# Folding 64-bit weights with ScalarE's low bits written as 32-bit integers, sines and arctangents as separate operations, and a new recorded order, in an attention and rational-activation kernel on one core

## The chip, the core and the metric

The kernel runs on one core of a Trainium2 chip. The core has a matrix engine (TensorE, PE in the profile; PEld is its weight load), a vector engine (VectorE, DVE), a scalar engine (ScalarE, ACT), a general engine (GpSimd, POOL), and a queue that issues most transfers (SyncE, SP). Each takes its instructions in order and waits on semaphores for the others. The metric is device time of one execution in microseconds (us); lower is better.

## What is computed

A gated linear attention over 768 positions (4 batches, 8 heads, 48 channels), with a complex decay per position and channel, feeds a feed-forward layer whose activation is a ratio of two polynomials. Cut to what matters:

```
mag = sqrt(a_re^2 + a_im^2); scale = min(mag, 0.999) / (mag + 1e-6)
for t in range(768):                       # per batch and head
    S = a[t] * scale[t] * S + k[t] v[t]^T  # complex decay, 48 x 48 state
    y[t] = q[t] . real(S)
h = x @ w_in                               # x = y as 3072 x 384; w_in 384 x 2048
P = a0 + a1 h + a2 h^2 + a3 h^3
Q = 1 + |b0| |h| + |b1| h^2
out = (P / (Q + 1e-6)) @ w_out             # w_out 2048 x 384
```

The kernel gets `w_in` and `w_out` as 64-bit floats and takes each to 32 bits itself.

## The kernel before

The sequence is cut into 6 chunks of 128 positions; a chunk of one batch is a unit, 24 in all, taken in 12 pairs. For a pair, `norm` (L444), `angle` (L474) and `trig` (L496) turn the decays into running magnitudes and angles: roots, scans, an arctangent, sums of angles, sines and cosines. `outer` (L512) multiplies q and k with them, and sends the products `Q` through twelve transfers a pair into the tile `HQ`, which has channels on partitions. `attn` (L542) transposes (L555), computes scores (L566), values (L582) and states (L597) on PE; the result `xT` goes to `ffn` (L614), eight groups a pair: PE makes `ph` (L627), ACT and DVE evaluate the activation through tiles A1, A2, A3 and z into `g`, and PE sums `po` (L645). The activation's quotient uses a reciprocal square root (`ROOT`) on ACT, whose table is another than the one with sine and arctangent, so an `ACT_TABLE_LOAD` stands between them.

Ahead of this, `weights` (L405) takes 28 blocks of 64-bit weights to 32 bits with `fold` (L390): 12 of `w_in`, 512 wide, and 16 of `w_out`, 384 wide. A block arrives in a buffer `raw` (ring `g` with 4 buffers, or `wh0` to `wh2`) as pairs of 32-bit words, low and high. Before, a fold is four instructions: ACT's `Abs` of the high word into the weight tile (L398, shown as L343); the sign alone left in the high word, on DVE or POOL (L399, shown as L331); the top three bits of the low word written beside it as a 16-bit number, on ACT (L401) or DVE (L402); and one DVE operation that shifts the tile left by 3 and ors in the high word (L403, shown as L331). In each, the source or the target has one element per 8 bytes. The first `ffn` block needs the first blocks of `w_in`, and all folds have to be done in its course.

`rouse` (L603) puts matmuls without use between those of the first pairs (L609), so that PE has work there. The first two pairs (`WHOLE`) multiply in 32 bits; after `split` (L416) the weights stand as a high and a low part.

Instructions are registered in a `Plan` (L82) with engines that may run them (`ways`), and a table `ORDER` (L223) fixes in one sequence which comes when and on which engine. `list_schedule` (L131), the planner with costs, is not run while the table fits. Every `vec` instruction has line L331, every `scal` one L343, every scaled copy of `evac` or `line` on ACT L337; so the tiles tell them apart. At the end `values_ok` (L867) and `count` (L890) check what the fast path relied on; the result `bad` is loaded by all engines (L907), which then go to the slow path or to the end.

## Time and profile before

| | |
|---|---|
| three runs | 645.45, 649.0, 650.76 us; median 649.0 |
| the profiled execution | 647.0 us, of which its span 645.3 us |
| PE busy | 574.8 us (89%) |
| DVE busy | 573.4 us (89%) |
| ACT busy | 539.5 us (84%) |
| POOL busy | 220.2 us (34%) |
| mean granted TensorE clock | 0.988 |

The page takes one execution. Busy shares are means over stages with different limits, so stretches of the span are read apart: the stage ahead of the first `ffn` block (to 76.4 us), the two pairs in 32 bits (to 190 us), the steady pairs after them, and the end. The idle time before an instruction is put down to what came last. Matmuls are pipelined and their ends modelled.

### The profile page before, as it was taken

What the parts mean: (1) busy time and instruction counts of PE and PEld (TensorE: products, weight loads), DVE (VectorE), ACT (ScalarE), POOL (GpSimd) and SP (SyncE); (2) the same over time, 40 slices, a digit from 0 to 9 for tenths busy, and PEclk for the clock granted to TensorE, in tenths of its full rate; (3) what the DMA queues carried; (4) which work ended last, traced back from release to release, by engine and by line L of the source; (5) the groups of instructions that cost most, each with busy time, mean ns of one, the idle gap of its engine ahead of it and who ended that gap; (6) DMA issues with size and microseconds to landing.
All of it is one profiled execution on the core that took longest, in us unless ns stands there. A gap on an engine that the chain in (4) does not pass through costs nothing.

```text
span 645.3 us, 13131 instructions
## 1 busy us (share of the span) xinstructions
PE 574.8 (89%) x5028; PEld 531.9 (82%) x5028; DVE 573.4 (89%) x996; ACT 539.5 (84%) x902; POOL 220.2 (34%) x202
## 2 busy tenths in 40 slices
PE   0037899998999999999999899999999999999994
PEld 0026776776779999999999899989999999999993
DVE  8787899899999999989999999988999978887683
ACT  7997999898888888989989788878788797667781
POOL 1001142326448555353541442644323443010200
PEclk9997999998999999999999999999999999999998
DMA  8677514744063253561441723600440534400001
GB/s 301 236 213 185 169 46 106 158 92 100 25 136 107 74 107 74 91 140 56 82 104 58 148 90 66 131 34 27 123 107 19 132 58 103 78 2 27 0 25 30
DMA packets 39094, 62.27 MB, mean 96 GB/s; under 512 B 4464, under 2 KB 26224, under 8 KB 39024
## 3 DMA queue, kind: packets, MB, share of 16 engines
q1 hardware_dynamic: 39024, 61.36, 39.0%
q8 instruction: 41, 0.67, 0.4%
q14 instruction: 29, 0.24, 0.1%
HBM read 37.75 MB, written 4.72 MB: 66 GB/s over the span
## 4 chain that ended last, share of the span: by engine, by line
DVE 26%; PE 21%; ACT 14%; issue 5%; DMA 2%; POOL 1%; SPq 0%; ACTq 0%; DVEq 0%; POOLq 0%
DVE A L331 11%; PE po L645 8%; PE ph L627 8%; ACT z L343 5%; ACT A L343 4%; DVE z L331 4%; PE at L566 2%; PE at L582 2%; DVE g L331 2%; DVE MM L331 1%; PE at L597 1%; DVE ST L331 1%; DVE T L331 1%; DVE RU L331 1%; ACT L343 1%
## 5 line engine op out<-in xcount | busy, mean ns | idle before, releaser
L645 PE MATMUL po<-wh,g 128*128 128x384 f32 x640 | 179.9, 340 | 0.4 <-DVE g L331 0.4
L627 PE MATMUL ph<-xT,wiH 128*128 128x256 f32 x960 | 162.2, 287 | 0.9 <-DVE A L331 0.8
L331 DVE SCALAR_TENSOR_TENSOR A<-A,co,z 128x512 f32<-128x512 f32 x176 | 130.9, 743 | 27.4 <-ACT z L343 24.7
L645 PE MATMUL po<-wo,g 128*128 128x384 f32 x428 | 146.5, 385 | 3.5 <-DVE g L331 3.5
L627 PEld LDWEIGHTS ph<-xT,wiH 128*128 128x128 f32 x960 | 135.7, 190 | 3.7 <-DVE A L331 2.3
L627 PE MATMUL ph<-xT,wi 128*128 128x256 f32 x632 | 122.7, 312 | 0.6 <-ACT A L343 0.5
L645 PEld LDWEIGHTS po<-wh,g 128*128 128x128 f32 x640 | 117.0, 188 | 3.1 <-issue 1.8
L331 POOL TENSOR_TENSOR g<-A,g 128x512 fp32r<-128x512 f32 x47 | 63.8, 1359 | 140.4 <-ACT g L692 77.3
L343 ACT ACTIVATE z<-A,co 128x512 f32<-128x512 f32 x96 | 66.3, 690 | 48.5 <-DVE A L331 44.3
L627 PEld LDWEIGHTS ph<-xT,wi 128*128 128x128 f32 x632 | 99.6, 190 | 7.0 <-ACT A L343 0.9
L645 PEld LDWEIGHTS po<-wo,g 128*128 128x128 f32 x428 | 80.1, 189 | 17.6 <-DVE g L331 4.6
L331 DVE SCALAR_TENSOR_TENSOR A<-A,co,ph 128x512 f32<-128x512 f32 x96 | 70.8, 740 | 2.6 <-ACT A L343 2.3
L343 ACT ACTIVATE A<-A,co 128x512 f32<-128x512 f32 x96 | 69.3, 722 | 2.2
L331 DVE SCALAR_TENSOR_TENSOR z<-A,z 128x512 f32<-128x512 f32 x96 | 66.7, 694 | 2.6
L343 ACT ACTIVATE A<-ph,co 128x512 f32<-128x512 f32 x96 | 64.7, 681 | 4.8 <-DVE A L331 3.8
L343 ACT ACTIVATE A<-ph 128x512 f32<-128x512 f32 x96 | 56.9, 592 | 4.6 <-PE ph L627 2.3
L566 PE MATMUL at<-HQ 96*128 96x128 f32 x384 | 51.9, 283 | 6.6 <-ACT kT L337 6.0
L343 ACT ACTIVATE z<-z 128x512 f32<-128x512 f32 x96 | 56.1, 584 | 1.8
L566 PEld LDWEIGHTS at<-HQ 96*128 96x128 f32 x384 | 48.8, 197 | 9.0 <-ACT kT L337 7.4
L609 PE MATMUL po<-Q,cmask 128*128 128x256 f32 x28 | 9.7, 489 | 42.2 <-DVE Q L331 42.2
L331 POOL TENSOR_TENSOR RU<-MM,RU 128x384 f32<-128x384 f32 x13 | 13.7, 1051 | 88.3 <-DVE RU L331 88.3
L609 PEld LDWEIGHTS po<-Q,cmask 128*128 128x128 f32 x28 | 6.7, 256 | 43.7 <-issue 42.2
(175 smaller groups left out, 1011.0 us busy)
## 6 DMA issues: line engine op xcount, KB each, us to landing
HQ<-Q SPq DMA_DIRECT2D x144, 128.0 KB, 4.5
AA<-in_aa SPq DMA_DIRECT2D x23, 384.0 KB, 3.9
QK<-in_qk SPq DMA_DIRECT2D x23, 384.0 KB, 4.9
V<-in_v SPq DMA_DIRECT2D x24, 256.0 KB, 5.0
g<-in_w_in SPq DMA_DIRECT2D x6, 512.0 KB, 5.7
wh<-in_w_in SPq DMA_DIRECT2D x6, 512.0 KB, 5.3
g<-in_w_out SPq DMA_DIRECT2D x8, 384.0 KB, 4.7
wh<-in_w_out SPq DMA_DIRECT2D x8, 384.0 KB, 3.8
```

Source lines behind the costliest of these rows:

```text
L331: call = lambda e: getattr(e, kind)(*map(real, args), **{k: real(x) for k, x in kw.items()})
L343: plan.op(dict(ACT=(act(n, psum) + more, lambda e: e.activation(o(), i(), f, **kw))), r, w)
L566: e.matmul(pst[:, i, :], hf[:, 4 * g + i, 1, :], hf[:, 4 * g + i, 0, :], start=True, stop=True)
L582: e.matmul(py[32 * y:32 * y + 32, min(j, 2), :], l, sts[h // 4][:, h % 4, :] if q is None else hf[:, h, 0, :], start=q is None and j == 0, ...
L597: e.matmul(pd[0:96, h], kT[:, h], V[:, VP * h:VP * h + D], start=True, stop=True)
L609: plan.op(dict(PE=(430, lambda e, x=x: e.matmul(idle[:, 0:2 * C], cmask, x(), start=True, stop=True)), SP=(0, lambda e: None)), (w,), ((id ...
L627: e.matmul(ph[:, x * T:x * T + T].rearrange("p (h t) -> p h t", h=nb), wt[f // 4 * NJ + j][:, f % 4 * P:f % 4 * P + P], xT[:, x0:x0 + nb, ...
L645: e.matmul(po[b][:, 0:DM], gg, wt, start=(f == 0 and n == 0), stop=(f == NFF - 1 and n == len(prods) - 1))
```

## The change

1. In `fold`, the second and third instruction are replaced by one operation, which the table puts on an engine. On ACT it reads the same 16-bit halves, at the same step of 8 bytes, and writes the top three bits into the low word as a 32-bit integer. On DVE or POOL it is the sign operation as before. DVE then has two operations in place of one: with ACT, shift-and-or with the low word, then the sign bit of the high word; without ACT, shift-and-or with the high word, then the low word shifted right by 29. The table puts 22 of 28 on ACT, 1 on DVE and 5 on POOL; before, ACT had 20 and DVE 8 of the third instruction, DVE 21 and POOL 7 of the second.
2. `trig`'s two sines and its arctangent are three operations of their own in place of one that couples them; each can stand anywhere in ACT's order.
3. The last pair's two results are evacuated whole, one by ACT and one by DVE, and sent by SP and by ACT's queue, in place of two halves each. The checks write over `fl` in place of a tile of the ring `A2`.
4. `ORDER` is another table.

```
         scal(AF.Abs, n, lambda: st.t, sign, (raw,), (st,), scale=2.0 ** -112)
-        vec("tensor_scalar", n, sign, sign, 0.0, 1.0, ALU.mult, ALU.mult, two=False, r=(raw,), w=(raw,), eng=EN["sign"])
-        top, units = (lambda y=y: raw.t.bitcast(U16)[:, :, y] for y in (1, 2))
-        plan.op(dict(ACT=(act(n), lambda e: e.activation(units(), top(), AF.Copy, scale=2.0 ** -13, bias=2.0 ** -14 - 0.5)),
-                     DVE=(dve(n, False), lambda e: e.tensor_scalar(units(), top(), 13, None, ALU.logical_shift_right))), (raw,), (raw,), port=True)
-        vec("scalar_tensor_tensor", n, i, i, 3, high, ALU.logical_shift_left, ALU.bitwise_or, r=(raw, st), w=(st,))
+        top = lambda: raw.t.bitcast(U16)[:, :, 1]
+        zero = lambda e: e.tensor_scalar(sign(), sign(), 0.0, 1.0, ALU.mult, ALU.mult)
+        p = plan.op(dict(DVE=(dve(n, False), zero), POOL=(pool(n, False), zero), ACT=(act(n), lambda e: e.activation(
+            low().bitcast(mybir.dt.int32), top(), AF.Copy, scale=2.0 ** -13, bias=2.0 ** -14 - 0.5))), (raw,), (raw,), port=True)
+
+        def first(e):
+            e.scalar_tensor_tensor(i(), i(), 3, low() if p.eng == "ACT" else high(), ALU.logical_shift_left, ALU.bitwise_or)
+
+        def second(e):
+            if p.eng == "ACT":
+                e.scalar_tensor_tensor(i(), high(), 1 << 31, i(), ALU.bitwise_and, ALU.bitwise_or)
+            else:
+                e.scalar_tensor_tensor(i(), low(), 29, i(), ALU.logical_shift_right, ALU.bitwise_or)
+
+        for f in (first, second):
+            plan.op(dict(DVE=(dve(n), f)), (raw, st), (st,), port=True)
...
-        keys = [t for t, _, _ in calls]
-        plan.op(dict(ACT=(2 * 1283 + len(calls) * act(2 * W), emit)), keys, keys)
+            table(AF.Arctan, lambda u=U[x]: u.T.t, U[x].T)
+
+    def table(f, x, key, **kw):
+
+        plan.op(dict(ACT=(act(2 * W), lambda e: e.activation(x(), x(), f, **kw))), (key,), (key,)).tab = 1
...
-                evac(n, lambda ob=ob, n=n: ob[:, 0:n], lambda o=o, cols=cols: o[:, cols], (o, "co"), ((ob, h),), -1.0 if plain else sc,
-                     ("ACT", "DVE")[h:h + 1] if end else None)
+            evac(DM, lambda ob=ob: ob[:, 0:DM], lambda o=o: o[:, 0:DM], (o, "co"), (ob,), -1.0 if plain else sc, ("ACT", "DVE")[b:b + 1] if end else None)
...
-        e.tensor_scalar(ok[:, 0], fl[:, 0], 2000.0, None, ALU.is_le)
+        e.tensor_scalar(fl[:, 1], fl[:, 1], -W, None, ALU.add)
+        e.tensor_tensor(fl[:, 1], fl[:, 1], fl[:, 1], ALU.mult)
+        for i, most in enumerate((2000.0, 0.09, 12.0)):
+            e.tensor_scalar(fl[:, i], fl[:, i], most, None, ALU.is_le)
```

What the table does is seen on the engines. On DVE, early in the program, before: the folds' sign operations (`TENSOR_SCALAR` on a raw buffer) among the scans of the first units' magnitudes (`MM`):

```order
L331 TENSOR_SCALAR g_118<-g_118 128x384
L331 TENSOR_SCALAR wh2_116<-wh2_116 128x384
L331 TENSOR_SCALAR g_114<-g_114 128x384
L331 SCALAR_TENSOR_TENSOR MM_168<-MM_168,ncar_93,Q_145 128x128
L331 SCALAR_TENSOR_TENSOR Q_145,fl_95<-kT_108,Q_145 128x384
L331 TENSOR_SCALAR wh0_121<-wh0_121 128x512
L331 SCALAR_TENSOR_TENSOR T_170<-SQ_141,T_170 128x384
L331 SCALAR_TENSOR_TENSOR wi2_166<-wi2_166,wh1_112 128x512
L331 SCALAR_TENSOR_TENSOR wo1_184<-wo1_184,wh2_116 128x384
```

The same place in the changed program, where L407 is `first` and L411 `second` of a fold:

```order
L407 SCALAR_TENSOR_TENSOR wi1_163<-wi1_163,g_110 128x512
L332 SCALAR_TENSOR_TENSOR T_161<-SQ_140,T_161 128x384
L407 SCALAR_TENSOR_TENSOR wo0_168<-wo0_168,g_114 128x384
L407 SCALAR_TENSOR_TENSOR wo1_180<-wo1_180,wh2_116 128x384
L332 SCALAR_TENSOR_TENSOR MM_146<-MM_146,ncar_93,SQ_140 128x128
L411 SCALAR_TENSOR_TENSOR wo0_168<-g_114,wo0_168 128x384
L411 SCALAR_TENSOR_TENSOR wi1_163<-g_110,wi1_163 128x512
L332 SCALAR_TENSOR_TENSOR MM_173<-MM_173,ncar_93,Q_143 128x128
L411 SCALAR_TENSOR_TENSOR wo1_180<-wh2_116,wo1_180 128x384
```

No sign operation stands ahead of ACT's share any more, and two 32-bit operations of two sources follow it. Counted ahead of the first activation operation of the first `ffn` block (`A3<-A3,co,ph`), DVE had 10 sign operations of 512 and 11 of 384, 2 of L402 of 384, and 10 shift-and-ors of 512 and 11 of 384; now it has 1 sign operation of 384, and 21 operations of two sources of 512 and 26 of 384. Of its other work there, six instructions stand later and two earlier. ACT has 21 of its 22 folds ahead of the first `A1<-ph` (10 of 512, 11 of 384), where it had all 20 (10 and 10). 11 useless matmuls of `rouse` are on PE in place of 17.

On ACT, in the steady pairs, before: sines and the arctangent follow one load, and the load for the root `z` comes after four activations that any table has:

```order
L507 ACT_TABLE_LOAD
L507 ACTIVATE T_1206<-T_1206 128x768
L507 ACTIVATE CO_1676<-CO_1676 128x768
L507 ACTIVATE T_1651<-T_1651 128x768
L343 ACTIVATE A3_2031<-ph_1997,co_82 128x512
L343 ACTIVATE A3_2041<-ph_1928,co_82 128x512
L343 ACTIVATE A1_2043<-ph_1928 128x512
L343 ACTIVATE A2_2054<-A1_2043,co_82 128x512
L343 ACT_TABLE_LOAD
L343 ACTIVATE z_2092<-A2_2054,co_82 128x512
```

The same place now, with the cosine (`CO`), the next pair's arctangent (`T_1615`) and the sine (`T_1180`) apart:

```order
L520 ACTIVATE CO_1664<-CO_1664 128x768
L344 ACT_TABLE_LOAD
L344 ACTIVATE z_1952<-A2_1919,co_82 128x512
L344 ACTIVATE z_1952<-z_1952 128x512
L344 ACTIVATE Z_1989<-RU_1910 128x384
L344 ACTIVATE A1_1998<-ph_1954 128x512
L520 ACT_TABLE_LOAD
L520 ACTIVATE T_1615<-T_1615 128x768
L344 ACTIVATE A3_2022<-ph_1954,co_82 128x512
L344 ACTIVATE A2_2032<-A1_1998,co_82 128x512
L520 ACT_TABLE_LOAD
L520 ACTIVATE T_1180<-T_1180 128x768
```

An arctangent that comes ahead of a sine has a load of its own. Over the fast path ACT had 31 loads and has 38; up to the third pair's first `A1` both have 15, so all seven come later.

## Rows read from the trace of the kernel before

**Rows 1.** The page: the span.
```profile
span 645.3 us, 13131 instructions
```
**Rows 2.** Stretches of the span: length, then busy time of each engine (instructions).
```profile
core 0: us, PE busy (x) PEld busy (x) DVE busy (x) ACT busy (x) POOL busy (x), PEclk, DMA share, GB/s
0.00:76.40 76.40, 27.77 (x199) 23.48 (x200) 60.17 (x146) 68.93 (x107) 6.96 (x17) 0.96 0.73 224
76.40:134.10 57.70, 54.96 (x316) 41.63 (x315) 53.38 (x96) 53.39 (x88) 19.05 (x22) 1.00 0.43 102
...
190.00:540.00 350.00, 342.93 (x3319) 332.40 (x3319) 328.82 (x547) 301.64 (x509) 148.44 (x127) 1.00 0.38 87
```
**Rows 3.** Stretches of 16 us ahead of the first ffn block.
```profile
16.00:32.00 16.00, 0.00 (x0) 0.00 (x0) 11.71 (x23) 15.91 (x22) 0.00 (x0) 1.00 0.69 239
32.00:48.00 16.00, 5.77 (x16) 4.25 (x16) 14.07 (x31) 15.94 (x24) 0.00 (x0) 1.00 0.77 210
48.00:64.00 16.00, 11.53 (x92) 10.19 (x92) 12.13 (x23) 12.71 (x18) 2.02 (x3) 0.79 0.79 179
```
**Rows 4.** DVE around the first activation operation: start, length, idle before.
```profile
76.43 0.75 DVE L331 SCALAR_TENSOR_TENSOR A<-A,co,ph 128x512 f32<-128x512 f32 x1
```
**Rows 5.** Waits, 0 to 76.4 us: who for whom, us, times, longest.
```profile
PE at L566 <- ACT kT L337: 5.5, 3, 3.6
...
DVE ST L331 <- PE at L566: 4.9, 3, 2.3
...
DVE wi L331 <- ACT wh L401: 1.7, 2, 1.3
...
DVE wo L331 <- ACT wh L401: 1.2, 2, 0.8
```
**Rows 6.** Fold operations by form: count, busy us, mean ns, idle before.
```profile
L401 ACT ACTIVATE wh<-wh 128x512 uint16<-128x512 uint16 x5 | 6.7, 1341 | 0.0
...
L401 ACT ACTIVATE wh<-wh 128x384 uint16<-128x384 uint16 x5 | 5.1, 1075 | 0.0
...
L331 DVE SCALAR_TENSOR_TENSOR wo<-wo,g 128x384 uint32<-128x384 uint32 x8 | 4.4, 552 | 0.8 <-ACT g L401 0.8
...
L343 ACT ACTIVATE wo<-wh 128x384 f32<-128x384 f32 x8 | 4.3, 543 | 0.0
...
L331 DVE SCALAR_TENSOR_TENSOR wi<-wi,g 128x512 uint32<-128x512 uint32 x6 | 4.1, 685 | 0.5 <-ACT g L401 0.5
...
L343 ACT ACTIVATE wi<-g 128x512 f32<-128x512 f32 x6 | 4.0, 668 | 0.0
...
L331 DVE TENSOR_SCALAR g<-g 128x384 f32<-128x384 f32 x6 | 2.1, 354 | 0.0
L331 DVE TENSOR_SCALAR wh<-wh 128x512 f32<-128x512 f32 x5 | 2.1, 420 | 0.0
...
L402 DVE TENSOR_SCALAR g<-g 128x384 uint16<-128x384 uint16 x3 | 1.8, 595 | 0.0
```
**Rows 7.** Table loads by line: count, busy us, mean ns, idle before.
```profile
L507 ACT ACT_TABLE_LOAD x15 | 19.2, 1283 | 0.3
L343 ACT ACT_TABLE_LOAD x15 | 19.2, 1283 | 3.6 <-DVE A L331 3.1 <-DVE g L331 0.3
```
**Rows 8.** The chain that ended last, 190 to 540 us: share by line.
```profile
by line: PE ph L627 14.2%; PE po L645 13.1%; DVE A L331 12.4%; issue 7.5%; ACT z L343 5.2%; DVE z L331 4.7%; ACT A L343 4.1%; PE at L566 3.4%; PE at L582 3.2%; DVE MM L331 2.6%; PE at L597 2.4%; DVE T L331 2.1%; ACT L343 1.5%; DVE ST L331 1
```
**Rows 9.** The end: start, length, idle before; and one whole evacuation by form.
```profile
635.74 0.94 ACT L337 ACTIVATE A<-po,co 128x192 f32<-128x192 f32 x2 [5.66 <-PE po L645]
...
636.79 0.74 DVE L331 TENSOR_SCALAR A<-po,co 128x192 f32<-128x192 f32 x2 [2.62 <-ACT A L337]
637.83 0.18 DVE L868 TENSOR_SCALAR A<-fl 128x24 f32<-128x24 f32 x1 [0.29 <-DMA out<-A]
...
639.07 0.14 DVE L892 TENSOR_SCALAR bad<-nok 1x1 int32<-1x1 f32 x1
...
L331 DVE TENSOR_SCALAR wo<-po,co 128x384 f32<-128x384 f32 x3 | 1.8, 613 | 0.4 <-PE po L645 0.4
```

More of the change, by code (lines that the diff above doesn't have):

```diff
@@ L342, in scal @@
     def scal(f, n, o, i, r, w, more=0, psum=False, **kw):
-        plan.op(dict(ACT=(act(n, psum) + more, lambda e: e.activation(o(), i(), f, **kw))), r, w)
+        p = plan.op(dict(ACT=(act(n, psum) + more, lambda e: e.activation(o(), i(), f, **kw))), r, w)
+        p.tab = 2 if f is ROOT else 0
     def pe(ns, fn, r, w):
@@ L496, in trig @@
     def trig(sines, arcs):
-        calls = []
         for x in sines[:1]:
             u = U[x]
-            calls += [(u.T, AF.Sin, {}), (u.CO, AF.Sin, dict(bias=math.pi / 2, scale=-1.0))]
+            table(AF.Sin, lambda u=u: u.T.t, u.T)
+            table(AF.Sin, lambda u=u: u.CO.t, u.CO, bias=math.pi / 2, scale=-1.0)
         for x in arcs[:1]:
-            calls.append((U[x].T, AF.Arctan, {}))
-        def emit(e):
-            for t, f, kw in calls:
-                e.activation(t.t, t.t, f, **kw)
-        keys = [t for t, _, _ in calls]
-        plan.op(dict(ACT=(2 * 1283 + len(calls) * act(2 * W), emit)), keys, keys)
+            table(AF.Arctan, lambda u=U[x]: u.T.t, U[x].T)
+    def table(f, x, key, **kw):
+        plan.op(dict(ACT=(act(2 * W), lambda e: e.activation(x(), x(), f, **kw))), (key,), (key,)).tab = 1
     def outer(c, bb):
@@ L701, in ffn @@
         for b, o in enumerate(po):
-            for h in range(2) if end else (0,):
-                n = DM // (2 if end else 1)
-                cols = slice(h * n, h * n + n)
-                ob = buf(ff, [P, 512], F32, *(("A2", A2B) if end or whole and b else ("wo15" if b else "ob", 1)))
-                evac(n, lambda ob=ob, n=n: ob[:, 0:n], lambda o=o, cols=cols: o[:, cols], (o, "co"), ((ob, h),), -1.0 if plain else sc,
-                     ("ACT", "DVE")[h:h + 1] if end else None)
-                dst = lambda b=b, cols=cols: out[c, b0 + b, :, cols].rearrange("o t m -> (o t) m")
-                dma(dst, lambda ob=ob, n=n: ob[:, 0:n], (ob,), (), 0.512 * n, 1000 if not end else 0)
+            ob = buf(ff, [P, 512], F32, *(("A2", A2B) if end or whole and b else ("wo15" if b else "ob", 1)))
+            evac(DM, lambda ob=ob: ob[:, 0:DM], lambda o=o: o[:, 0:DM], (o, "co"), (ob,), -1.0 if plain else sc, ("ACT", "DVE")[b:b + 1] if end else None)
+            dma(lambda b=b: out[c, b0 + b].rearrange("o t m -> (o t) m"), lambda ob=ob: ob[:, 0:DM], (ob,), (), 0.512 * DM,
+                1000 if not end else 0, eng=("SP", "ACT")[b:b + 1] if end else ("SP",))
     def run_ffn(*args, **kw):
@@ L896, in attn_moe @@
     plan.op(dict(DVE=(700, values_ok)), (*(("fl", i, n) for i in range(2) for n in range(NC * B)), *(("fl", 2, n) for n in range(0, NC * B, 2)),
-                                        *(("ncar", b) for b in range(B))), (("cnt", 0), ok), port=True)
+                                        *(("ncar", b) for b in range(B))), (("cnt", 0), "fl"), port=True)
     pc = buf(ps, [P, 512], F32, "at", 2)
```

99 lines of the change are left out of this document (48 added, 51 removed).

## The prediction

> **What bounds the kernel now.** I read the page for the span [rows 1], then the stretches of the span, because the means hide that the stages have different limits [rows 2]. Until 76.4 us, where DVE does the first activation operation of the first `ffn` block [rows 4], PE is busy 27.8 us of 76.4, while ACT is busy 68.9 and DVE 60.2 [rows 2]. After that PE is busy 55.0 of 57.7 us, and 342.9 of 350.0 from 190 to 540 us [rows 2]. So the reader is to see two kernels in one: a preparation that ends when ACT and DVE let it, and a long stretch in which PE has at most 2.7 and 7.1 us of idle time to give back. A time won ahead of the first block moves the whole of what follows; a time won on ACT or DVE after it is mostly hidden.
>
> In the preparation ACT is the bound: in two stretches of 16 us it is busy 15.91 and 15.94 us [rows 3]. The waits say the same. PE waits 5.5 us for kT, which ACT evacuates late since other work is ahead of it in its queue, then DVE waits 4.9 us for the scores of PE; and DVE waits 1.7 and 1.2 us for ACT's part of a fold [rows 5]. The activations of that part are the dearest there: 1341 ns for 512 elements and 1075 for 384, where `Abs`, which reads the same blocks at the same step of 8 bytes but as 32-bit words and writes 32-bit words, takes 668 and 543 [rows 6].
>
> **The folds on DVE.** Ahead of the first activation operation DVE had (counts by the order, means from [rows 6]) 10 x 0.420 + 11 x 0.354 for signs, 2 x 0.595 for L402, 10 x 0.685 + 11 x 0.552 for the shift-and-or: 22.2 us. It has 21 x 0.685 + 26 x 0.552 + 0.354 = 29.1. That is 6.9 more. Six other instructions go behind that point and two come ahead; four net, three priced as the 384-wide two-source row (0.55) and one, 768 wide, at twice that, give back 2.8. The new second operation shows in no row, but differs from the first only in its constants, so I price it by the same rows; were it to cost less, it could not go under the one-source sign operation (0.354 and 0.420, 23 times: 5.1 to 6.1 less). DVE's work to that point is thus 60.2 + 6.9 - 2.8 = 64.3 us, 4.1 more than before [rows 2].
>
> **The folds on ACT.** No row shows a 16-bit read with a 32-bit write. The nearest from above is L401 itself (1341 and 1075 ns), the nearest from below `Abs` on the same blocks (668 and 543) [rows 6]. ACT had 10 x 1.341 + 10 x 1.075 = 24.2 us and has 21 folds: 10 x 1.341 + 11 x 1.075 = 25.2 at the upper price (+1.0), 10 x 0.668 + 11 x 0.543 = 12.7 at the lower (-11.5). I take the lower. L401 costs 2.1 ns for each element more (266 ns for 128), `Abs` 1.0 (125 for 128), and what the two share is the step of 8 bytes on the reading side; the 16-bit write at that step is found in L401 alone and is taken away. Against it: the 16-bit read is also found in L401 alone, and stays. So this is a choice, and both ends stay in the range.
>
> The Trainium skill speaks to this price. Its page "ScalarE: Activation LUTs", section "Step-by-step: what each stage is for", says that an activation runs one element per cycle, 0.833 ns, for any function, in 32 and 16 bits alike; by that the new operation would cost the lower price. The trace does not agree for the 16-bit operation that it shows (2.1 ns), so the page gives my choice no weight.
>
> **What the preparation gains.** At the lower price ACT has 68.9 - 11.5 = 57.4 us ahead of the first block, under DVE's 64.3; DVE is then the bound, and the question is how much of its 16.2 us of idle time (76.4 - 60.2) is left. Of this, 4.9 + 1.7 + 1.2 = 7.8 hang on ACT's queue by [rows 5]; they go. 8.4 are left in smaller waits (on transfers at the start, on scans, on ACT again); with ACT 7 us ahead I let 1.7 more go. 64.3 + 6.7 = 71.0, so 5.4 us earlier than 76.4. Bounds: half of these 6.7 go too, 67.7 (-8.7); none of the 16.2 goes, 80.5 (+4.1). Three of the first twelve `HQ` transfers are now issued by ACT and wait there for `Q` of DVE; behind them in ACT's queue stand folds that DVE reads a few instructions later, so ACT's new lead is partly spent there, which is why I don't go to the lower bound. The 11 useless matmuls in place of 17 fill PE's idle time and cost nothing; if their lack leaves PE longer at the lower of its two clock levels, the stretch of 16 us with a mean clock of 0.79 [rows 3] shows the size: 16 x 0.42 = 6.7 us at 1.2 GHz, in which at most 3.4 us of PE's work is lost once.
>
> **The split tables.** 7 more loads at 1.283 us are 9.0 us of ACT, all behind the third pair's first `A1`. PE is the bound there and ACT is busy 301.6 of 350 us [rows 2]: the cover is 48 us of idle time on ACT. Not all is covered: the roots `z` that wait for the load are on the chain. ACT's lines have 5.2 + 4.1 + 1.5% of it there, about 11% [rows 8]; 11% of 9.0 is 1.0, and I take 1.5, as a load stands right ahead of `z`. The bounds are 0 (the separate operations also break up the block of load, three activations and load, which would be a gain of its own) and 9.0.
>
> The Trainium skill has a rule against this part. Its page "ScalarE: Activation LUTs", section "What ACT_TABLE_LOAD costs", adds to the 1283 ns a drain of some 1380, 2.66 us for each switch. By that the seven would be 18.6 us and my 11% 2.0. The trace does not agree: 30 loads have 0.3 + 3.6 us of idle time ahead of them in all [rows 7], 0.13 each, so the sum goes by 9.0.
>
> **The end.** Now ACT evacuates two halves from 635.74, DVE's halves wait 2.6 us for them to start at 636.79, the checks wait for a transfer to free their tile and start at 637.83, and `bad` is there at 639.07 + 0.14 = 639.21 [rows 9]: 3.5 us. Changed: one evacuation of 384 on DVE (0.613 [rows 9]) beside ACT's, then the checks with no transfer ahead of them. From 637.83 to 639.21 they take 1.4; two more small ones at 0.08 make 1.5. 3.5 - 0.6 - 1.5 = 1.4 less. It counts in full, as all engines read `bad` last.
>
> **The sum.** 647.0 (the profiled execution; its span is 645.3) - 5.4 + 1.5 - 1.4 = 641.7. The three runs have a median 2.0 above that execution, and the change is stated against it: 649.0 - 5.3 = **643.7 us**. Other swaps of engines by the table (a few evacuations from DVE to ACT, a few products to POOL) are under 3 us on each engine over the whole and lie under PE.
>
> **The rivals.** *B: the read sets the price, and it is hidden.* ACT's folds stay at 1.341 and 1.075. ACT remains the bound, 1.0 longer, and DVE's 4.1 more fit into its 16.2 us of idle time: 649.0 + 1.0 + 1.5 - 1.4 = 650.1. For it: ACT's saturation [rows 3]. *C, the other side: the read sets the price, and DVE's extra work comes behind ACT's.* Place: `first` stands in DVE's queue waiting for ACT's fold, and behind it the products `Q` that PE's first work waits for; already now DVE waits there [rows 5]. Then ACT's 1.0 and DVE's 4.1 add: 649.0 + 5.1 + 1.5 - 1.4 = 654.2, and 661.7 if the loads count in full with ACT as the bound. It ends over 655.5 (1% slower) once the loads cost over 2.8. Against it: DVE's idle time of 16.2 us is large. *D: the separate tables help.* The block of load, sines, arctangent and load holds `z` up for two loads (2.6 us [rows 7]) and its activations; in pieces it holds it up less at a time, and PE gets back what it idles in the steady pairs, at most 7.1 us [rows 2]: with half of that and no cost of loads, 649.0 - 5.4 - 3.5 - 1.4 = 638.7. Against it: the seven loads.
>
> **How the numbers follow.** A (the forecast) 0.58, B 0.12, C 0.20, D 0.10. A measurement of this kernel can tell about 1% (6.5 us) from no change. A runs from -8.7 to +4.1 around its term and from 0 to 9.0 in the loads, so from 636 to 652 most of the time: of its 0.58, 0.32 are under 642.5, 0.24 within 1%, 0.02 above. B gives 0.10 within and 0.02 above; C 0.04 within and 0.16 above; D 0.10 under. Faster 0.42, same 0.38, slower 0.20. The range goes from 634 (below it only the best of D) to 655 (above it the upper part of C).
>
> **What would show it.** In the profile after: the mean of L403's rows, 0.67 and 0.54 for A, 1.3 and 1.1 for B and C, with the turn at about 1.0; the L407 and L411 rows at 0.69 and 0.55; the first `A<-A,co,ph` on DVE near 71 us; DVE no longer idle for ACT's folds; 37 loads besides the first, with PE still busy 98% from 190 to 540 us; `bad` some 2 us behind the last `po`. I am wrong if ACT's folds stay dear, if ACT waits at its `HQ` transfers so long that DVE idles again, or if PE's idle time in the steady pairs grows by more than 5 us.

## The result, and the profile after

The changed kernel takes 631.43 us (median, 630.88 to 633.35), the kernel before in the same comparison 648.87. The ratio is 0.974, with a 95% interval of 0.970 to 0.979: faster, by 17.4 us where 5.3 were forecast, and below the forecast range. The profiled execution takes 630.88 us. One execution of the kernel before, out of 63 in the later comparisons, took 1576 us and is not counted in the ratios.

The page of the changed kernel: span, busy time and share of each engine, and the granted clock in 40 slices.
```profile
span 629.2 us, 13110 instructions
...
PE 570.5 (91%) x5016; PEld 527.4 (84%) x5016; DVE 563.0 (89%) x982; ACT 541.3 (86%) x916; POOL 227.1 (36%) x208
...
PEclk9998999999999999999999999999999999999998
```
Stretches of the changed kernel, cut at the same places of the work as [rows 2]: up to the first activation operation on DVE, one pair on, two pairs on, and the steady pairs; then two stretches ahead of the first block as in [rows 3].
```profile
0.00:71.30 71.30, 27.31 (x194) 21.51 (x195) 64.41 (x146) 61.90 (x110) 6.29 (x16) 0.98 0.76 240
71.30:124.50 53.20, 52.45 (x308) 39.76 (x308) 51.25 (x92) 51.58 (x87) 24.84 (x27) 1.00 0.44 123
124.50:168.50 44.00, 44.00 (x348) 35.13 (x347) 41.91 (x73) 41.34 (x73) 27.39 (x24) 1.00 0.49 92
190.00:540.00 350.00, 344.73 (x3321) 334.22 (x3320) 323.66 (x539) 307.66 (x511) 142.16 (x121) 1.00 0.38 85
...
16.00:32.00 16.00, 1.19 (x2) 0.50 (x2) 15.57 (x30) 14.83 (x29) 0.00 (x0) 1.00 0.92 310
32.00:48.00 16.00, 5.67 (x19) 4.13 (x20) 14.33 (x28) 14.55 (x24) 0.00 (x0) 1.00 0.72 178
```
The preparation ends where it was forecast to end: at 71.3 us, not 76.4, ACT is no longer full in it, and DVE, at 64.4 us, is the engine with the most work. ACT, at 61.9 us, is closer behind than the 57.4 of the forecast. What was not forecast stands in the second and third line. The kernel before needed 57.7 us for the first of these pairs [rows 2] and, in a stretch that the prediction's rows leave out, 51.0 for the second:
```profile
134.10:185.10 51.00, 48.80 (x371) 38.48 (x370) 47.21 (x74) 45.74 (x80) 25.56 (x25) 0.97 0.46 93
```
So 5.1 us were won ahead of the first block and 11.5 more in these two pairs. These are the pairs whose weights are still 32-bit, while the folds, the products and the attention of the next pair run beside them. PE's waits there, first of the kernel before (76.4 to 185.1 us), then of the changed one (71.3 to 168.5 us): who waits for whom, us, times, longest.
```profile
PE po L645 <- DVE g L331: 3.5, 4, 1.3
PE at L597 <- DVE ST L331: 0.6, 1, 0.6
...
```
```profile
PE po L655 <- DVE g L332: 0.7, 1, 0.7
```
And DVE's queue at the first block, before and after: start, length. In the old order three steps of folds (two L402 and a shift-and-or) and the product `T` stand between the block's operations, so that its first `g`, for which PE's output matmuls wait, starts at 80.46 us, 4.0 us after the first `A`. In the new order the chain stands together and `g` starts 2.1 us after `A`, 7.0 us earlier than before.
```profile
77.09 0.74 DVE L402 TENSOR_SCALAR g<-g 128x512 uint16<-128x512 uint16 x1
77.62 0.58 DVE L331 SCALAR_TENSOR_TENSOR wo<-wo,wh 128x384 uint32<-128x384 uint32 x1
78.12 0.54 DVE L331 SCALAR_TENSOR_TENSOR T<-SQ,T 128x384 f32<-128x384 f32 x1
78.59 0.74 DVE L331 SCALAR_TENSOR_TENSOR A<-A,co,z 128x512 f32<-128x512 f32 x1
79.25 0.59 DVE L402 TENSOR_SCALAR g<-g 128x384 uint16<-128x384 uint16 x1
79.62 0.80 DVE L331 SCALAR_TENSOR_TENSOR z<-A,z 128x512 f32<-128x512 f32 x1
80.46 0.75 DVE L331 SCALAR_TENSOR_TENSOR g<-A,co,z 128x512 f32<-128x512 f32 x1
```
```profile
71.28 0.72 DVE L332 SCALAR_TENSOR_TENSOR A<-A,co,ph 128x512 f32<-128x512 f32 x1
71.92 0.74 DVE L332 SCALAR_TENSOR_TENSOR A<-A,co,z 128x512 f32<-128x512 f32 x1
72.69 0.69 DVE L332 SCALAR_TENSOR_TENSOR z<-A,z 128x512 f32<-128x512 f32 x1
73.42 0.75 DVE L332 SCALAR_TENSOR_TENSOR g<-A,co,z 128x512 f32<-128x512 f32 x1
```
The fold operations and the table loads of the changed kernel, answering to [rows 6, 7] (count, busy us, mean ns, idle before):
```profile
L403 ACT ACTIVATE wh<-wh 128x512 int32<-128x512 uint16 x5 | 3.3, 666 | 0.0
...
L403 ACT ACTIVATE wh<-wh 128x384 int32<-128x384 uint16 x6 | 3.3, 547 | 0.0
```
```profile
L407 DVE SCALAR_TENSOR_TENSOR wo<-wo,g 128x384 uint32<-128x384 uint32 x8 | 4.4, 553 | 0.0
...
L411 DVE SCALAR_TENSOR_TENSOR wi<-wh,wi 128x512 uint32<-128x512 uint32 x5 | 4.2, 843 | 0.0
...
L407 DVE SCALAR_TENSOR_TENSOR wi<-wi,g 128x512 uint32<-128x512 uint32 x6 | 4.1, 687 | 0.0
```
```profile
L520 ACT ACT_TABLE_LOAD x21 | 26.9, 1283 | 0.4
L344 ACT ACT_TABLE_LOAD x16 | 20.5, 1283 | 0.9 <-DVE MM L332 0.7
```
The end, answering to [rows 9]: ACT and DVE evacuate one tile each, the checks follow at once, and `bad` is there at 623.42.
```profile
620.80 0.58 ACT L338 ACTIVATE A<-po,co 128x384 f32<-128x384 f32 x1 [5.22 <-PE po L655]
...
621.27 0.62 DVE L332 TENSOR_SCALAR A<-po,co 128x384 f32<-128x384 f32 x1 [2.12 <-PE po L655]
...
621.80 0.17 DVE L871 TENSOR_SCALAR fl<-fl 128x24 f32<-128x24 f32 x1
...
623.28 0.14 DVE L895 TENSOR_SCALAR bad<-nok 1x1 int32<-1x1 f32 x1
```

### The profile page after: what moved, and what is told of

Read it like the earlier page. It is cut to its first block, busy times and chain, and to the rows that moved or that the text cites. A ratio compares the mean times of both kernels' runs of the same rounds, so it can differ in the third digit from the quotient of the medians.

```text
span 629.2 us, 13110 instructions
## 1 busy us (share of the span) xinstructions
PE 570.5 (91%) x5016; PEld 527.4 (84%) x5016; DVE 563.0 (89%) x982; ACT 541.3 (86%) x916; POOL 227.1 (36%) x208
## 4 chain that ended last, share of the span: by engine, by line
PE 29%; ACT 28%; DVE 28%; issue 5%; DMA 5%; POOL 2%; SPq 1%; ACTq 0%; DVEq 0%; POOLq 0%
DVE A L332 12%; PE ph L637 10%; PE po L655 10%; ACT A L344 7%; ACT z L344 7%; DVE z L332 4%; PE at L576 3%; PE at L592 3%; DVE T L332 2%; DMA QK<-in_qk 2%; ACT L520 2%; PE at L607 2%; DMA g<-in_w_out 2%; DVE MM L332 2%; ACT T L520 1%
## 5 line engine op out<-in xcount | busy, mean ns | idle before, releaser
L332 POOL TENSOR_TENSOR g<-A,g 128x512 fp32r<-128x512 f32 x49 | 67.7, 1383 | 157.0 <-ACT g L702 85.0
L576 PE MATMUL at<-HQ 96*128 96x128 f32 x384 | 50.0, 277 | 0.5 <-ACT kT L338 0.4
L332 POOL TENSOR_TENSOR QK<-QK,RU 128x768 f32<-128x768 f32 x19 | 35.7, 1879 | 39.4 <-DMA QK<-in_qk 21.9
L576 PEld LDWEIGHTS at<-HQ 96*128 96x128 f32 x384 | 47.0, 191 | 3.4 <-ACT kT L338 1.9
L332 POOL TENSOR_TENSOR Z<-MM,Z 128x384 f32<-128x384 f32 x13 | 13.6, 1043 | 63.8 <-ACT Z L344 63.8
L332 DVE TENSOR_TENSOR ST<-at,cmask 128x512 f32<-128x512 f32 x48 | 32.2, 682 | 3.4 <-PE at L576 3.3
```

The costliest lines, as they stand in the source:

```text
L332: call = lambda e: getattr(e, kind)(*map(real, args), **{k: real(x) for k, x in kw.items()})
L576: e.matmul(pst[:, i, :], hf[:, 4 * g + i, 1, :], hf[:, 4 * g + i, 0, :], start=True, stop=True)
```

## The experiments

**A measure of progress.** Since the kernels do the same PE work in other orders, I compare them by it: each matmul is counted with the mean time to the next start that its kind has in the changed kernel (long gaps, in which PE waits, are not in that mean), the useless ones (`rouse`) and the second copies of the last two kernels with nothing, 529.8 us in all. The table says by how much a kernel's profiled execution had done the same amount earlier (-) than the kernel before, which reaches 4, 28, 60, 100 and 500 us of it at 62.0, 102.4, 150.0, 203.1 and 607.3 us. The two 32-bit pairs lie between the first and the fourth mark. The medians and ratios are of 4 to 10 executions, each against the kernel before run beside it (647.5 to 648.9 us); the marks are of one execution, which can lie some us from its kernel's median.

```
                            median us  ratio, 95% interval       4    28    60   100   500
changed                       631.43   0.974 (0.970 to 0.979)  -6.4  -8.7 -11.2 -15.6 -15.0
new_ops_old_order             645.18   0.995 (0.993 to 0.996)  -4.9  -2.2  -2.0  -3.3  -3.6
old_folds_new_order           638.22   0.985 (0.982 to 0.989)  -1.9  -3.2  -4.5  -8.9  -8.8
new_to_first_pair             646.33   0.997 (0.995 to 0.999)  -7.2  -1.0  -1.5  -2.2  -1.9
new_to_second_pair            635.34   0.979 (0.976 to 0.982)  -6.0  -7.9  -8.9  -9.8  -8.6
new_to_third_pair             631.18   0.974 (0.970 to 0.978)  -6.9  -9.7 -11.2 -13.8 -14.6
new_to_fourth_pair            633.60   0.977 (0.974 to 0.981)  -6.6  -8.8 -10.4 -14.7 -12.0
new_sequence_old_engines      660.06   1.019 (1.016 to 1.022)  -6.6  -5.2  -1.8  +1.0 +12.3
old_sequence_new_engines      664.19   1.026 (1.022 to 1.030)  -2.5  -1.1  +2.1  +7.0 +10.7
products_back_on_vector       640.17   0.988 (0.985 to 0.991)  -7.3  -7.6  -4.5  -7.1  -6.0
tables_together               640.27   0.987 (0.984 to 0.990)  -7.0 -10.3  -3.9  -8.2  -5.1
steady_tables_together        633.29   0.978 (0.974 to 0.982)  -7.1  -9.3 -11.2 -15.6 -13.1
pair1_sines_together          638.80   0.986 (0.983 to 0.988)  -6.4  -4.7  -3.6  -6.0  -4.5
old_order_rouse_moved         646.04   0.996 (0.993 to 0.999)  -4.6  -0.1  -0.3  +0.3  +3.1
old_order_rouse_and_chain     647.22   0.999 (0.997 to 1.002)  -4.8  -2.3  -2.2  -3.3  -3.3
no_rouse                      638.04   0.985 (0.982 to 0.989)  -6.0  -4.8  -6.6 -10.3  -9.3
changed_more_rouse            630.78   0.976 (0.971 to 0.981)  -7.0  -9.6 -12.2 -16.3 -15.9
before_wait_filled            644.20   0.993 (0.991 to 0.995)  -1.4  -1.4  -1.6  -3.6  -5.5
changed_wait_filled           633.59   0.979 (0.974 to 0.983)  -7.2  -9.6 -11.6 -14.8 -13.0
```

In the edits below NEW is the changed kernel's list of (operation, engine), OLD the same operations at the places and on the engines that their counterparts have in the kernel before, and `to(p)` the place of the first feed-forward operation of pair p (the first pair is 0).

### Price or order

```diff
-ORDER = NEW
+ORDER = OLD
```


> The changed kernel's instructions (int32 fold on ScalarE, two scalar_tensor_tensor, trig calls as single operations, checks, whole tail) put into the order and the engine choices of the kernel before: each fold step stands where its counterpart stood, sines and arctangent of a block stand together again. Theory A, arrangement: the 10 us beyond the forecast, which the trace shows between the first outer block (A<-A,co,ph at 71 us) and the third pair (168 us), come from the new order of the two 32-bit pairs; the cheaper fold gives only some of the 5 us ahead of the first block. Then this kernel takes 640 to 647 us. Theory B, price: ScalarE's released time (22 folds, 0.55 to 0.68 us each, 13 us) is what moved that stretch, in whatever order. Then it takes 630 to 637 us.

```diff
-            low().bitcast(mybir.dt.int32), top(), AF.Copy, scale=2.0 ** -13, bias=2.0 ** -14 - 0.5))), (raw,), (raw,), port=True)
+            units(), top(), AF.Copy, scale=2.0 ** -13, bias=2.0 ** -14 - 0.5))), (raw,), (raw,), port=True)
...
-            e.scalar_tensor_tensor(i(), i(), 3, low() if p.eng == "ACT" else high(), ALU.logical_shift_left, ALU.bitwise_or)
+            if p.eng == "ACT":
+                zero(e)
...
-                e.scalar_tensor_tensor(i(), high(), 1 << 31, i(), ALU.bitwise_and, ALU.bitwise_or)
...
+            e.scalar_tensor_tensor(i(), i(), 3, high(), ALU.logical_shift_left, ALU.bitwise_or)
```


> The changed kernel's order and engine choices, with the fold at its old price: where ScalarE takes the low bits it writes 16-bit halves again (1.34/1.07 us), VectorE's first step is the sign in place (0.42/0.35 us) and one scalar_tensor_tensor follows; the other folds are wholly the old ones. It leaves the low three bits of the weights out where ScalarE does them, since sign and bits would have to stand the other way round. Theory A, arrangement: 631 to 637 us (13 us of ScalarE time come back, spread over folds of which most lie beside a bound TensorE or before it, and VectorE gets 5 us back). Theory B, price: 641 to 649 us, the old time.

The first took 645.2 us, as theory A has it. The second took 638.2, 1.2 us over A's range and 2.8 under B's, so nearer to A. The new operations alone bring 3.6 us, the new order alone 10.6, both together 17.4. Both kernels have the new end, so what it brings, some 1 us, is in the 3.6 and in the 10.6. The old price comes back in full (count, busy us, mean ns):
```profile
L403 ACT ACTIVATE g<-g 128x512 uint16<-128x512 uint16 x5 | 6.8, 1367 | 0.0
```
and costs 6.8 us in the new order, 4.5 of them ahead of the first block: the lead at the first mark is 1.9 us in place of 6.4, and from there on this kernel gains 6.9 us up to the fifth, against 8.6 with the cheap folds. In the old order the cheap folds bring 4.9 us at the first mark, too, but 2.9 of these are gone ten microseconds later.

### Which part of the order

```diff
-ORDER = NEW
+ORDER = NEW[:to(p)] + [x for x in OLD if x not in NEW[:to(p)]]
```
with p = 0, 1 and 2 in turn.


> The changed kernel's instructions; its new order only up to the first operation of the first pair's feed-forward part (preparation and first attention), the old order from there on. Theory A, arrangement of the two 32-bit pairs: the 5 us of the preparation are kept and the 10 us behind it are lost, 641 to 645 us. Theory B, price, or a gain that is all in the preparation: 630 to 636 us.

> The changed kernel's instructions; its new order and engines up to the first operation of the second pair's feed-forward part, and from there on the old order. The new order only up to the first pair's took 646.3 us, up to the third pair's 631.2. If the gain lies in pair 0 (where the folds, pair 1's attention and the blocks share DVE and ACT), this one takes 631 to 636 us; if it lies in pair 1 (TensorE waits of 0.76 and 1.37 us for g, and a second stretch at half the clock at 155 us), 641 to 646 us; in both alike, 637 to 640.

> The changed kernel's instructions; its new order up to the first operation of the third pair's feed-forward part, and from there on the old order (sines and arctangents together, old places of loads and evacuations). The trace says that all 15 us are won by the third pair (-16.6 us at 168 us) and that the steady pairs bring nothing. Theories A and B both give 629 to 636 us. If the steady pairs' order held a gain or a loss of its own that the progress table hides, it comes out above 638 or below 628 us.

The cuts give 646.3 us (1.3 over the range of theory A, far from B), 635.3 and 631.2. The order of the first pair is worth 11 us, that of the second some 4 (the intervals of the ratio just overlap), that of all the others nothing. The first of them is the most telling: it has the whole preparation of the new order, and at the first mark the largest lead of all three, 7.2 us; by 16 us of the work it is down to 0.8. The trace shows where it went. The stretches 70 to 76 and 76 to 84 us, and the wait of PE in them:
```profile
70.00:76.00 6.00, 2.87 (x14) 2.18 (x12) 5.97 (x14) 5.91 (x11) 0.00 (x0) 1.00 0.50 158
76.00:84.00 8.00, 6.11 (x14) 4.29 (x15) 7.39 (x12) 6.03 (x11) 2.73 (x5) 0.57 0.39 131
```
```profile
PE po L654 <- DVE g L331: 5.0, 1, 5.0
```
DVE and ACT are full (5.97 and 5.91 of 6.00 us) with what the old order puts between the block's operations; PE, which had arrived early, waits 5.0 us for the first `g`, and is then at half its clock (0.57). Here a lead of PE ahead of the first block was worth nothing, since DVE and ACT did not have it too.

Two repairs of the old order were meant to show one of these causes by itself.

```diff
-six rouse operations: SP (no operation), three others: PE
+the six: PE, right behind the first scores, the three others: SP (no operation)
```


> The changed kernel's instructions in the old order, as in new_ops_old_order (645.2 us), with one repair: six of the useless matmuls that keep TensorE busy are switched on behind the first scores (TensorE idles there from 52.9 to 55.4 us and then works at half its clock up to 68 us: granted 0.57 and 0.79), and three that stand among real work (at 51, 60 and 65 us) are switched off. Theory K, the clock: the lead of 4.9 us that this order has at the first feed-forward matmul and that is down to 2.0 us ten us later is lost to the half clock; then the kernel takes 641 to 643 us. Theory W, the wait: whatever PE wins there it hands back at the first output matmul, which waits for g of the first block, since DVE and ACT have folds, T and A in their queues ahead of it (g<-A,co,z at 80.5 us in the kernel before, 73.4 in the changed one); then 644.5 to 646 us.

```diff
-DVE: A(block 0), fold, fold, T, A, fold, z, g
+DVE: A(block 0), fold, A, z, g, fold, T, fold
```


> The kernel of old_order_rouse_moved with a second repair: on DVE the first block's chain A, A, z, g stands together; two fold steps and one product T (1.8 us) that stood in it come behind g, as do two evenly small ACT steps. By theory K this brings nothing more (641 to 643 us); by theory W it brings up to 1.8 us more than the first repair alone (g of the first block 1.8 us earlier, 642.5 to 644.5 us), and a good part of the 14 us between the two orders is still missing, since the same pattern stands in the later blocks of the pair.

They took 646.0 and 647.2 us, against 645.2 without, the second outside both theories: inconclusive. In the first kernel's profiled execution the half clock was not taken away but came later (granted 0.50 from 64 to 72 us), so it does not test theory K. Its ten executions differ: the four with a mean granted clock of 0.991 or more took 642.0 to 644.3 us, the other six 645.9 to 649.8, which speaks for a part of K. In the profiled execution of the second, at 643.1 us one of its fastest, the granted clock is 1.00 from 40 to 88 us and the first `g` comes at 75.6 us (78.1 without the repairs); the lead of 4.0 us at 16 us of the work is 2.3 at 22, since PE then waits 2.3 us for `A` and 1.3 for `g`. There, what one block gains alone the next one's queue takes back.

### Sequence or engines

```diff
-ORDER = NEW
+ORDER = [(op, old engine of op) for op, _ in NEW]
```


> The changed kernel's instructions in its new sequence, but each of the 163 operations that the new order gives to another engine goes back to the engine that it had (of these 39 stand between the first pair's and the third pair's feed-forward part, with 17 moved from DVE to POOL and 9 back). Two theories of what in the new order wins the 10 us behind the first block. S, sequence: pair 1's attention comes forward (its first transposes 112.4 to 100.9 us) and folds and products stand so that TensorE never runs dry. Then 631 to 636 us. G, engines: the products given to GpSimd (QK<-QK,RU: 2 to 5, Q<-QK,CO: 1 to 3) free 5 to 7 us of VectorE, which TensorE waited for. Then 638 to 645 us.

```diff
-ORDER = OLD
+ORDER = [(op, new engine of op) for op, _ in OLD]
```


> The mirror image: the changed kernel's instructions in the sequence of the kernel before, with the engine choices of the new order. S, sequence: 641 to 648 us, as with the old engines (645.2) or worse, since an operation that was placed for one engine now stands in another's queue. G, engines: 633 to 640 us.

660 and 664 us: both theories missed, and the question can't be decided in this way. A sequence and the engines that it was made for belong together. A smaller cut tells more:

```diff
-15 operations of outer and norm between to(0) and to(2): POOL
+the same 15: DVE
```


> The changed kernel in its new sequence; only 15 operations between the first and the third pair's feed-forward part that the new order gives to GpSimd (8 products of the outer step, 3 of the norm, 3 norm vectors and the like) go back to VectorE, where they were: some 11 us more for VectorE in a stretch of 97 us in which it is idle for 4. With all 163 engine choices undone the kernel took 660 us. If VectorE's load is what the two 32-bit pairs hang on, 637 to 643 us; if TensorE bounds them and VectorE has room, 631 to 633.

640.2 us, 8.7 more than the changed kernel. Up to the second mark little is lost; then PE waits (71.2 to 130.1 us), and of the 7.6 us of lead 5.3 are gone at 34 us of the work:
```profile
PE po L655 <- DVE g L332: 5.1, 2, 4.0
```
The longest of these waits, 3.97 us, costs more than itself: the four output matmuls behind it took 2.71 us, at half the clock (granted 0.57 from 104 to 108 us), where four take 1.45 at 94.78 us of the same trace. So VectorE's load is a part of what bounds these pairs, although TensorE is busy 98.6% of the first in the changed kernel (52.45 of 53.20 us).

### Sines and arctangents

```diff
-step 737: sine of CO, step 745: sine of T, step 754: arctangent of T (next pair)
+steps 745 to 747: sine of T, sine of CO, arctangent of T (next pair)
```
This is one group; the first kernel does it to all but one, the second to those from the fourth pair on, and the third has only pair 1's two sines (steps 259 and 404) moved together, to 368.

> The changed kernel with sines and arctangent of a pair side by side again in ScalarE's queue for all groups but the last one of three, at the place of the middle one; all else in the new order. Six table loads fewer, 6 x 1.283 = 7.7 us of ScalarE. Forecast's reading (each load costs the time some 11 to 17% of itself): 0.8 to 1.3 us faster, 630 us. Loads wholly hidden: 631.4. The split helps by itself, as the block of loads holds up the roots z: 633 to 637.

> The changed kernel with sines and arctangent side by side only from the fourth pair on (eight groups); the two 32-bit pairs and the third are in the new order as they are. Five table loads fewer, 6.4 us of ScalarE. The kernel with all groups together lost 9 us, of which its trace puts 8 between 102 and 137 us and 1 to 3 behind 180 us. Theory of the forecast (loads on the chain at 11 to 17%): 630.3 to 630.7, not to be told from 631.4. Loads hidden and grouping harmless: 631.4. Grouping holds up the roots z in the steady pairs too: 633 to 635.

> The changed kernel with only the second pair's two sines put side by side, at the earliest place where both can stand; the new order has the sine of CO 145 steps ahead of the sine of T. If what the kernel with all groups together lost between 102 and 112 us (6 us) comes from this group, since CO's products and pair 1's attention wait for it, this one takes 636 to 639 us; if not, 631 to 632.

640.3, 633.3 and 638.8 us. In the steady pairs five loads fewer bring no gain; the result is 1.9 us over the changed kernel. That lies in the range of the theory that the grouping holds up the roots, but the two intervals of the ratio overlap, so it can't be told from no change. The first kernel lost more than any of its theories had; by its size (7.4 of 8.9 us) the loss is mostly that of pair 1. ACT's queue there, in the third kernel (start, length, idle before):
```profile
93.45 1.28 ACT L520 ACT_TABLE_LOAD   x1
95.99 0.84 ACT L520 ACTIVATE T<-T 128x768 f32<-128x768 f32 x1 [1.25 <-DVE T L332]
96.74 0.58 ACT L344 ACTIVATE A<-ph 128x512 f32<-128x512 f32 x1
...
98.33 1.28 ACT L344 ACT_TABLE_LOAD   x1
...
103.25 0.84 ACT L344 ACTIVATE SQ<-AA 128x768 f32<-128x768 f32 x1 [1.85 <-POOL ncar L332]
```
The sine waits 1.25 us for its argument and a square 1.85 us for POOL; the block's `A` stand behind them, and PE waits 2.8 us for `A` and 3.0 for `g`. Behind each of these waits the granted clock is 0.50 for 3.4 us (from 88.9 and from 106.0 us). This says that the new order hangs on the freedom to set the two sines 145 steps apart. It does not say that the old order lost as much by having them together, since it was laid out around that.

### The clock

```diff
-            for h in range(H):
+            for h in [*range(7 if (c, bb) == (1, 0) else 0), *range(H)]:
```


> The kernel before, with one of its state products computed twice: 7 of the 8 small matmuls that end at 153.5 us are issued a second time (1.1 us of TensorE, the same result), into the 1.2 us in which TensorE waits there for g. If the drop to half the clock at 155.4 to 158.8 us (granted 0.79 in 152 to 160 us) comes from TensorE's idle stretches ahead of it, it is gone and 1.7 us are won in that stretch (about 647 us); if it stays, the kernel takes 648 to 650 us.

The same edit in the changed kernel:

> The control for before_wait_filled (4.4 us won): the same 7 matmuls issued twice, in the changed kernel, where TensorE neither waits nor drops to half the clock between 144 and 168 us. If their gain came from the clock, they are pure work here, at most 1.1 us: 631.5 to 632.5 us. If issuing them twice helps by itself (by delaying what follows), 627 to 630 us.

Seven useless matmuls more made the kernel before 4.4 us faster, and the changed kernel 2.2 us slower. PE in the kernel before, then with the wait filled:
```profile
152.23 1.48 PE L597 MATMUL at<-V,kT 128*96 128x48 f32 x16
154.92 2.48 PE L645 MATMUL po<-wo,g 128*128 128x384 f32 x4 [1.21 <-DVE g L331]
157.33 1.78 PE L582 MATMUL at<-ST,V 128*32 128x128 f32 x32
```
```profile
150.64 2.67 PE L597 MATMUL at<-V,kT 128*96 128x48 f32 x30
153.34 1.56 PE L645 MATMUL po<-wo,g 128*128 128x384 f32 x4
154.82 1.08 PE L582 MATMUL at<-ST,V 128*32 128x128 f32 x32
```
After the wait of 1.21 us the same four output matmuls took 2.48 us, and 1.56 where there was no wait; the granted clock of 152 to 160 us was 0.79 and is 1.00. The first `ph` behind this stretch, in the two traces:
```profile
159.92 0.48 PE L627 MATMUL ph<-xT,wi 128*128 128x256 f32 x1
```
```profile
156.71 2.86 PE L627 MATMUL ph<-xT,wi 128*128 128x256 f32 x12
```
It starts 3.2 us earlier, where the lead ahead of the edit was 1.6 (this execution had the clock up earlier at the start: 0.50 for 3.4 us, against 6.8). So the stretch itself won 1.6 us, about the 1.7 that were expected. The lead grows to 5.5 us behind 200 us, where the edit does nothing; why, the two traces don't show, and of the median's 4.4 us only these 1.6 are traced to the edit. In the changed kernel the same seven matmuls cost 1.2 us at their place (the trace is 0.4 us ahead of the changed kernel's at 118 us and 0.8 behind at 143), which is their work. So delay by itself wins nothing; another 1 us was lost behind 365 us. The median lies over both ranges, and its interval overlaps that of the changed kernel.

```diff
-11 rouse operations: PE, the others: SP (no operation)
+all rouse operations: SP (no operation)
```


> The changed kernel with its 11 useless matmul operations all left out (TensorE then idles about 4 us more ahead of the first block). The forecast took them for free and bounded the clock's price at 3.4 us. If the clock of the start is a part of what the new order holds, TensorE stays at half its clock into the first feed-forward matmuls: 633 to 636 us. If they do nothing: 631.4; if they stand in the way of real work: 630.

638.0 us, 6.6 more, and 2 over the range for the clock. The first `A<-A,co,ph` comes at 75.2 us, 3.9 later than in the changed kernel. PE's scores of the second batch, without and with the useless matmuls:
```profile
59.61 3.78 PE L576 MATMUL at<-HQ 96*128 96x128 f32 x16 [0.79 <-ACT kT L338]
```
```profile
59.24 2.05 PE L576 MATMUL at<-HQ 96*128 96x128 f32 x16
```
By these durations PE worked at the lower level without them, up to where the trace's first clock record stands, at 67.7 us.

```diff
-three rouse operations: SP (no operation)
+the three: PE, right behind the first scores
```


> The changed kernel, all its own order, with three more useless matmuls switched on behind the first scores, where TensorE idles from 51.7 to 53.3 us before it works at half its clock until 57 us. Leaving all of them out cost 6.6 us. If the rest of the half-clock stretch can be had back: 630 to 631 us (0.5 to 1.2 us under the changed kernel); if the useless matmuls hold kT up instead: 632 us.

630.8 us: the half-clock stretch at 54 to 57 us is gone (granted 1.00), and the time is the same. What was left of the half clock in the preparation was hidden.

### A version of the best stretches

```diff
-ORDER = NEW
+ORDER = NEW[:to(3)] + [x for x in OLD if x not in NEW[:to(3)]]
-two rouse operations: SP (no operation)
+the two: PE, right behind the first scores
```


> A version put together from the best stretches: the new order up to the fourth pair's feed-forward part, where the trace of the changed kernel leads by 15.8 us, the old order from there on, in which the kernel new_to_third_pair kept its lead unchanged; and two more useless matmuls switched on at 52 us, where TensorE idles 1.6 us before it drops to half the clock. Expected 629.5 to 630.5 us, 1 to 2 us under the changed kernel.

633.6 us, 2.2 more than the changed kernel where 1 to 2 less were expected: the lead of 14.9 us at 120 us of the work is 13.4 at 140 and 12.0 at 280. No version that was tried beats the changed kernel by what can be measured.

## Why the prediction was wrong

**What was right.** The price of the new activation was taken from the row of `Abs`, 0.668 and 0.543; it is 0.666 and 0.547. So the 16-bit write at a step of 8 bytes was the dear part, not the read. The second operation on DVE costs what the first does (0.686 and 0.687 us at 512, 0.548 and 0.553 at 384). One of them took 1.50, which makes the mean of 0.843 in the row shown. ACT falls below DVE in the preparation, DVE's work up to the first block is 64.4 us (forecast 64.3), and the first `A<-A,co,ph` comes at 71.3 us (forecast 71.0). At the end 3.5 us from the first evacuation to `bad` became 2.6 (620.80 to 623.42): 0.9 less, 1.4 were forecast.

**What was right by its result alone.** ACT's sum of 57.4 us ahead of the first block came out at 61.9. It took the rows' means for the time that a fold holds the queue, but these overlap what follows: an L401 is followed by the next start after 1.11 us on average (512) and 0.87 (384), an L403 after 0.61 and 0.46. So the folds gave back some 8.7 us and not 11.5; and roundings of `wi` (`wiH`), a sine and the first root stand earlier than before. It did no harm, as DVE was still the engine with more work.

**The step that failed** is the first one: that after 76.4 us PE has only 2.7 us in the first pair and 7.1 in the steady ones to give back, so that "a time won ahead of the first block moves the whole of what follows" and a time won on ACT or DVE behind it "is mostly hidden"; with it the line that the other moves of the table "lie under PE", at nothing. The measured size of that term is 13.8 us (645.2 - 631.4, the same operations in both orders); with the old folds the new order brings 10.6, the new end included. Three things were wrong in it.

First, the stretch from 134 to 190 us is left out of the rows and of the argument. PE idled 2.2 us in it, and it has the second half-clock stretch.

Second, busy is not bound. In these two pairs together PE was busy 103.8 of 108.7 us (95.5%), DVE 100.6 (92.5%) and ACT 99.1 (91.2%). Three engines so close to full, in a cycle in which PE waits for `g`, `g` for `z` and `A`, and these for PE, are held up by each other's queue order, and the idle time of each is only what the cycle lost at that engine. This is a reading; what the runs show of it are single places, such as the 5.0 us that PE waited for `g` in new_to_first_pair and the 4.0 in products_back_on_vector.

Third, PE's busy time was taken as fixed work. From 10 to 100 us of PE's work the kernel before takes 130.0 us and the changed one 120.7 for the same 90.0 us of work:
```profile
73.10:203.10 130.00, 124.28 (x844) 97.00 (x846) 120.46 (x206) 117.36 (x201) 57.38 (x59) 0.99 0.47 108
```
```profile
66.80:187.50 120.70, 119.95 (x804) 95.35 (x802) 114.54 (x202) 116.15 (x204) 64.56 (x63) 1.00 0.48 118
```
Of the 9.3 us, 5.0 are PE's idle time (5.7 to 0.7) and 4.3 are busy time for the same work. Some 1.6 of these are the half-clock rows above (0.92 in four output matmuls, 0.70 in the values; filling the wait in the old order won 1.6 back, too), 0.4 a useless matmul at 76.8 us; where the other 2.3 lie, spread over `po` and `ph`, stays open. DVE has 5.9 us less and POOL 7.2 more in it.

**The sum as it came out**, in the profiled executions: 6.3 us up to 10 us of PE's work (the preparation; forecast 5.4), 9.3 from there to 100 (forecast nothing), 0.6 lost again in the steady pairs (15.6 at 100, 15.0 at 500), and 1.1 behind the last output matmul (9.1 us to the end of the span became 8.0; forecast 1.4): 16.1, the difference of the spans.

**The tables.** 1.5 us were charged for seven loads. Taking five of them out again brought nothing, new_to_third_pair with 30 loads takes 631.2 us, and in pair 1 the separate sines are what the new order needs. Rival D had the direction (separate tables help) but looked for it in the steady pairs, where nothing was found that can be told from no change, and priced it inside PE's idle time. The 37 loads have 1.3 us of idle time ahead of them, 0.04 each. The Trainium skill's page "ScalarE: Activation LUTs", section "What ACT_TABLE_LOAD costs", has a drain of some 1380 ns with each load; this trace does not agree either.

**The clock.** The prediction bounded the lack of six useless matmuls at 3.4 us. That was not run by itself; leaving out the eleven that are left costs 6.6, so the useless matmuls are worth more than PE's lost work counted once. Late scores and states hold up the other engines, too: without the useless matmuls DVE is busy 4.68 of 8.00 us from 56 to 64 us and ACT 5.30 from 64 to 72, against 5.85 and 7.94 in the changed kernel.

**The rivals and the range.** B and C fell with the price of the activation. The range ended at 634 since every case in it took the shift of the first block as all that could be won; a case in which the reordering of the two 32-bit pairs matters was missing.

What stays open: which of the new order's moves in these pairs carries how much, and how much of it goes by the clock. Sequence and engines could not be taken apart, and the two repairs of the first pair's old order brought nothing that the medians show.

## What to carry to other kernels

Read every stretch, and where three engines are each over 90% busy in a cycle, don't price a new order of their queues at nothing because one of them is busy 95% of the time: compare the time for the same amount of that engine's work. A lead that one engine gets ahead of such a stretch holds only if the queues it meets there have it, too. A wait of TensorE can cost the clock behind it, as those of 1.2, 3.0, 4.0 and 5.0 us did here; a few useless matmuls put into such a wait are a cheap trial, but where there is no wait they cost their time.

## What the runs showed of the hardware

- A ScalarE activation that writes 16-bit values at a step of 8 bytes took 1367 ns for 512 elements a partition (1341 in the kernel before), the one that reads the same 16-bit values and writes 32-bit words 666.
- The granted clock of a profile can read 1.00 in a stretch in which TensorE's matmuls take nearly twice as long: 16 scores took 3.78 us at 59.61 in the kernel without useless matmuls, where the column reads 1.00 from 56 to 64 us, and 2.05 in the changed one. In that trace the first clock record stands at 67.7 us; ahead of it, durations tell more than that column.
- One kernel's executions differ by their clock. Over 62 executions of the kernel before, the time and the mean granted clock (0.981 to 0.993) are correlated with -0.67, 3.3 us for 0.01; the changed kernel's executions lie at 0.993 to 0.997. By that slope some 3 us of the 17.4 go with the clock; a correlation does not say which causes which.
- Behind a wait, four output matmuls took 2.93 us (wait of 5.02 us, new_to_first_pair), 2.93 (3.01, pair1_sines_together), 2.71 (3.97, products_back_on_vector) and 2.48 (1.21, the kernel before), against 1.56 without a wait; a granted clock of 0.50 begins between 1.4 us before and 0.5 us after their start. Not every wait does this: behind one of 1.29 us at 81.26 in the kernel before, four took 1.56.
